# Sharing the start of a kernel out anew: first sequence's k and v in long runs, its p on ScalarE's queue, its mix on TensorE

## Chip, cores and metric

The kernel runs on one core of one Trainium2 chip. The metric is the device time of one execution in microseconds.

## What is computed

For each of 8 batches and 8 heads (S = 576 positions of D = 64) a packed attention, then a channel mix over the heads side by side (512 channels):

```python
def sm_attn(qq, kk, vv):                    # softmax(qq kk' / 8) vv
    ...
p_packed = sm_attn(p, k, v)                 # p: 32 rows a head
x = sm_attn(q, p_packed, p_packed)          # then heads side by side: [8, 576, 512]
x_prev = x shifted by one position, zero first
xk = mu_k * x + (1 - mu_k) * x_prev
xr = mu_r * x + (1 - mu_r) * x_prev
out = sigmoid(xr @ w_r) * (relu(xk @ w_k) ** 2 @ w_v)
```

The inputs mu and w are float64 and reach the chip as pairs of 32-bit words; q, k, v, p are float32. w_k is [512, 1024], w_v [1024, 512], w_r [512, 512].

## The kernel before, in words

A planner (`Flow`) runs generators with ranks and estimated times and emits the instructions in that order; the order on each engine is fixed when the kernel is built. Tiles come from pools with a set count of slots (`take`, `give`).

*Attention of one batch.* k and q arrive head by head, in pieces of 64 floats (256 bytes) for batches 0 and 1 (`loads`), are turned on TensorE (`transposed_on_pe`, L387) and copied to SBUF by ScalarE (kT, qT). p arrives in four loads (`packed`, L407) and is turned on VectorE (`pt`, L416). `front` makes the scores of p against k (L437); `weights_of` takes the maximum and exp and turns the result (L520, aT); L461 sums v with it; VectorE scales that to `pm`; its transpose ppT meets q in `back` (s2, L541). `back` ends with eight VectorE steps and exp (L553 to L576), of which a2 comes, and px (L584) is x transposed, 128 channels at a time; `mixed_in` copies it to `xt`.

*Channel mix.* Positions are cut into 9 chunks of 512. `mix` forms mu * x + (1 - mu) * x_prev, one scaled copy on ScalarE (L639), one scale-add on VectorE (L643); `split` makes a high and a low part (L659 on ScalarE, L661 on VectorE), so that three fast matmuls stand for one exact one. `gates` (L717 to L719) are 16 units of three matmuls, `keys` (L678 to L680) 32, `values` (L746 to L748) 32 per chunk.

*Weights.* `convert` loads a [128, 512] piece of float64 (SP, L207) into a `sq` slot, and turns it into a high and a low part: ScalarE scales the upper words (L285, `m`), VectorE shifts (L287), merges the sign (L289) and the low bits (L291), ScalarE casts the high part (L295), VectorE subtracts (L297). There are 4 pieces of w_r, 8 of w_k, 8 of w_v, 2.27 us of VectorE each. The parts of w_v have tiles of their own.

*The start.* TensorE has nothing but batch 0's attention until the first mix is done, and the planner fills it with matmuls on `spare` (L817). All loads go out on SP's queue, k of batch 0 first, then p, v, q, w_r. A load takes the semaphore of the eighth load before it, so that at most eight are in flight.

Of the kernel before, what the change touches and what calls it, by code (L numbers as in the profile page):

```python
# [163 lines left out]
def attn_pack_channel_mix(ctx: ExitStack, tc: tile.TileContext, q, k, v, p, mu_k, mu_r, w_k, w_v, w_r, out):  # L164
# [48 lines left out]
    LANDS = 2.0  # L213
    T6 = S // 6
# [49 lines left out]
    wv_h = const.tile([P, NF, DM], F32R, name="wv_h")  # L264
    wv_l = const.tile([P, NF, DM], F32R, name="wv_l")

    def convert(w, hi, lo, c, o, n, event, first=None):
# [4 lines left out]
        staged = yield from flow.take("staged")  # L272
        slot = yield from flow.take("sq")
        st = tile_([P, 2 * WP], U32, "sq", slot, "st")
        yield from load(st[:, :2 * n], w[c * P:(c + 1) * P, o:o + n].bitcast(U32), 0.46, 3.5e-3 * n)
# [93 lines left out]
    def transposed_on_pe(tag, b, pr, raw_space, raw_slot, raw):  # L369

        yield from reached()
        kq = yield from flow.take("kq")
# [473 lines left out]
```

## Time and profile before

| | us |
|---|---|
| median of 3 runs | 606.32 (605.44 to 607.43) |
| span of the profiled execution | 605.1 |
| TensorE busy in it | 593.7 |
| VectorE, ScalarE busy | 363.9, 331.0 |

The profile has no time of its own for the profiled execution beside its span; the median stands 1.2 us above the span. The busy time of TensorE counts `spare` matmuls, and ends of matmuls are modelled, so a busy stretch is read with its lines. Times in the rows are from the start of the span.

### The profile page before, as it was taken

Reading aid. Unit: us, or ns where it says so; the run is one execution under the profiler, and the core shown is the slowest. Engines: PE = TensorE matmul, PEld = TensorE weight load, DVE = VectorE, ACT = ScalarE, POOL = GpSimd, SP = SyncE. Lnnn points to the kernel's source line nnn. Section 1 sums busy time; section 2 is a strip of 40 time slices with the busy share of each in tenths; the row PEclk is TensorE's granted clock in tenths of the full one; section 3 lists DMA queues with packets and bytes.
Section 4 is the critical chain, followed back from the end, with each engine's and each line's share of the span. In section 5 each row is a group of like instructions: output and inputs, shape, how many; then the busy total and the mean of one; then the engine's idle time right before and its main releaser. Section 6 shows DMA issues by size and latency. Waiting matters only on the chain.

```text
span 605.1 us, 10174 instructions
## 1 busy us (share of the span) xinstructions
PE 593.7 (98%) x3984; PEld 471.1 (78%) x3984; DVE 363.9 (60%) x701; ACT 331.0 (55%) x579; POOL 2.1 (0%) x23
## 2 busy tenths in 40 slices
PE   8899999999999999999999999999999999999997
PEld 7787777777777777777877787778788888888886
DVE  1499999949688479556765577166503822451321
ACT  4478784775774648454845485457534803641420
POOL 0000000000000000000000000000000000000000
PEclk9899999999999999999999999999999999999999
DMA  8895561764634646346034702000010010001001
GB/s 189 248 266 136 216 155 34 166 126 88 113 60 137 118 70 139 99 74 143 1 103 64 144 1 72 20 1 0 26 45 1 0 70 0 2 0 71 0 2 69
DMA packets 159184, 49.43 MB, mean 82 GB/s; under 512 B 143776, under 2 KB 151968, under 8 KB 159136
## 3 DMA queue, kind: packets, MB, share of 16 engines
q1 hardware_dynamic: 159136, 48.79, 34.0%
q8 instruction: 31, 0.51, 0.3%
q14 instruction: 17, 0.14, 0.1%
HBM read 39.33 MB, written 9.44 MB: 81 GB/s over the span
## 4 chain that ended last, share of the span: by engine, by line
PE 84%; DVE 5%; ACT 4%; SPq 3%; DMA 2%; issue 1%; ACTq 0%
PE pvo L746 11%; PE ph L678 10%; PE pvo L747 10%; PE pvo L748 10%; PE ph L680 10%; PE ph L679 10%; PE pr L717 5%; PE pr L719 5%; PE pr L718 5%; SPq L207 3%; PE pa L461 2%; PE pa L584 2%; DMA st<-in_moe_w_r 1%; PE pa L541 1%; ACT x L639 1%; DVE m L289 1%
## 5 line engine op out<-in xcount | busy, mean ns | idle before, releaser
L678 PE MATMUL ph<-xk,wk_h 128*128 128x512 f32 x288 | 114.8, 399 | 0.0
L746 PE MATMUL pvo<-wv_h,sq 128*128 128x512 f32 x288 | 113.9, 395 | 0.0
L679 PE MATMUL ph<-xk,wk_h 128*128 128x512 f32 x288 | 112.4, 390 | 0.0
L680 PE MATMUL ph<-xk,wk_l 128*128 128x512 f32 x288 | 112.3, 390 | 0.0
L747 PE MATMUL pvo<-wv_l,sq 128*128 128x512 f32 x288 | 112.3, 390 | 0.0
L748 PE MATMUL pvo<-wv_h,sq 128*128 128x512 f32 x288 | 112.2, 390 | 0.0
L689 ACT ACTIVATE r<-ph 128x512 f32<-128x512 f32 x72 | 43.0, 598 | 90.7 <-PE ph L680 89.7
L696 DVE CAST sq<-r 128x512 fp32r<-128x512 f32 x72 | 30.3, 420 | 100.6 <-ACT r L692 98.4
L746 PEld LDWEIGHTS pvo<-wv_h,sq 128*128 128x128 f32 x288 | 54.1, 188 | 15.9 <-issue 4.5
L678 PEld LDWEIGHTS ph<-xk,wk_h 128*128 128x128 f32 x288 | 54.1, 188 | 15.5 <-issue 4.5
L643 DVE SCALAR_TENSOR_TENSOR x<-xt,mus,x 128x512 f32<-128x512 f32 (+7 forms) x128 | 60.4, 513 | 6.0 <-ACT x L639 5.9
L680 PEld LDWEIGHTS ph<-xk,wk_l 128*128 128x128 f32 x288 | 54.1, 188 | 11.5
L748 PEld LDWEIGHTS pvo<-wv_h,sq 128*128 128x128 f32 x288 | 54.1, 188 | 11.4
L639 ACT ACTIVATE x<-xt,mus 128x512 f32<-128x512 f32 (+7 forms) x128 | 62.0, 530 | 1.5 <-DVE xr L661 1.3
L747 PEld LDWEIGHTS pvo<-wv_l,sq 128*128 128x128 f32 x288 | 54.1, 188 | 10.7
L679 PEld LDWEIGHTS ph<-xk,wk_h 128*128 128x128 f32 x288 | 54.2, 188 | 10.3
L717 PE MATMUL pr<-wr_h,xr 128*128 128x512 f32 x144 | 58.7, 408 | 0.0
L719 PE MATMUL pr<-wr_h,xr 128*128 128x512 f32 x144 | 56.7, 394 | 1.0 <-DVE xr L661 1.0
L718 PE MATMUL pr<-wr_l,xr 128*128 128x512 f32 x144 | 56.3, 391 | 0.0
L728 ACT ACTIVATE sig<-pr 128x512 f32<-128x512 f32 x36 | 21.3, 601 | 60.1 <-PE pr L719 56.5
L698 DVE TENSOR_TENSOR sq<-r,sq 128x512 fp32r<-128x512 f32 x72 | 49.4, 686 | 1.4
L757 DVE TENSOR_TENSOR sig<-pvo,sig 128x512 f32<-128x512 f32 x36 | 23.9, 686 | 38.8 <-PE pvo L748 38.8
(80 smaller groups left out, 727.5 us busy)
## 6 DMA issues: line engine op xcount, KB each, us to landing
out<-sig SPq DMA_DIRECT2D x36, 256.0 KB, 2.1
vt<-in_v SPq DMA_DIRECT2D x16, 512.0 KB, 4.6
raw<-in_k SPq DMA_DIRECT2D x96, 72.0 KB, 2.8
raw<-in_q SPq DMA_DIRECT2D x96, 72.0 KB, 2.8
st<-in_moe_w_k SPq DMA_DIRECT2D x8, 512.0 KB, 6.0
st<-in_moe_w_v SPq DMA_DIRECT2D x8, 512.0 KB, 5.5
raw<-in_k SPq DMA_DIRECT2D x16, 144.0 KB, 2.9
raw<-in_q SPq DMA_DIRECT2D x16, 144.0 KB, 5.1
```

Of the source, the lines that this page charges most:

```text
L639: nc.scalar.mul(x32[:, o:o + n], xts[b, c][:, 1 + s:1 + s + n], mus[:, j, c:c + 1])
L643: nc.vector.scalar_tensor_tensor(x32[:, o:o + n], xts[b, c][:, s:s + n], mus[:, j + 1, c:c + 1], x32[:, o:o + n], op0=ALU.mult, op1=ALU.add,)
L678: nc.tensor.matmul(ph, wk_h[:, c, fs], xh, start=(c == 0), stop=False)
L679: nc.tensor.matmul(ph, wk_h[:, c, fs], xl, start=False, stop=False)
L680: nc.tensor.matmul(ph, wk_l[:, c, fs], xh, start=False, stop=(c == NC - 1))
L698: nc.vector.tensor_tensor(hl[:, 1, :], r, hl[:, 0, :].bitcast(F32), op=ALU.subtract)
L717: nc.tensor.matmul(pr, xh[:, ts_], wr_h[:, c, :], start=(c == 0), stop=False)
L718: nc.tensor.matmul(pr, xh[:, ts_], wr_l[:, c, :], start=False, stop=False)
L719: nc.tensor.matmul(pr, xl[:, ts_], wr_h[:, c, :], start=False, stop=(c == NC - 1))
L746: nc.tensor.matmul(pv[t], sh, wv_h[:, f, :], start=(f == 0), stop=False)
L747: nc.tensor.matmul(pv[t], sh, wv_l[:, f, :], start=False, stop=False)
L748: nc.tensor.matmul(pv[t], sl, wv_h[:, f, :], start=False, stop=(f == NF - 1))
```

## The change

Four things, all in the start. (1) k and v of batch 0 are loaded two heads at a time with six neighbouring positions to a partition, so in runs of 6 x 64 floats (1,536 bytes). VectorE puts k in the old order (`side`) ahead of the transposes, aT is made of six blocks of 96 to match v, and half of the qT copies move from ScalarE to VectorE. (2) w_r's first piece is loaded ahead of k, the second behind it; the four loads of batch 0's p and eight small new ones of mu (`mub`) go out on ScalarE's queue. (3) Batch 0's first chunk is no longer mixed on ScalarE and VectorE: mu goes into `pm` (`shared`: `pms`, two taps for each of xr and xk), and TensorE makes xr and xk directly from A (a2 with a zero column ahead, kept in halves hf = 0, 1), eight groups of eight matmuls; ScalarE casts the high part and VectorE subtracts, both from PSUM (`first_out`). The 64 positions left over are `kept` for the next chunk. Gates and keys wait for halves (`made`). (4) Weight pieces have eight `st` slots; w_v's two parts are written over the piece they came from. Conversions of w_k are `held` until both halves of A are there.

```diff
-    FIRST = 10.09, 10.29
+    FIRST = 9.97, 9.982, 10.07, 10.09
-    def load(dst, src, issue, us):
+    def load(dst, src, issue, us, beside=False):
+        if beside:
+            yield "scalar", 0.1, None, None
+            nc.scalar.dma_start(dst, src)
+            return
...
+                if b == 0 and tag == "kT":
+                    raw = tile_([P, 2, 6, D], F32, space, slot, "raw")
+                    yield from load(
+                        raw[:T6], src[b, 2 * pr:2 * pr + 2].rearrange("h (p c) d -> p h c d", p=T6), 0.4, 0.76,
+                    )
...
+            r2 = tile_([P, 6, 2 * D], F32, "raw", side, "side")
+            yield vec2(12 * D)
+            nc.vector.tensor_copy(r2[:T6].rearrange("p c (h d) -> p h c d", h=2), raw[:T6])
...
-            if beside:
+            if beside and hf:
                 yield act(HS)
                 nc.scalar.copy(t[:, hf * HS:(hf + 1) * HS], bank[:, :HS])
+            elif beside:
+                yield vec(HS)
+                nc.vector.tensor_copy(t[:, hf * HS:(hf + 1) * HS], bank[:, :HS])
...
+    def shared(sp, pm):
...
+        for j in (1, 0):
+            nc.vector.tensor_tensor(pms[:, j, 0], flat, mub[1][:, j], op=ALU.mult)
+            nc.vector.tensor_tensor(pms[:, j, 1], flat, pms[:, j, 0], op=ALU.subtract)
...
+    def first_mix():
...
+                        for pr in (2 * g, 2 * g + 1):
+                            own = slice(32 * pr, 32 * pr + 32)
+                            for h, half in enumerate(HALVES):
+                                o = 1 - tap + hf * HS
+                                nc.tensor.matmul(
+                                    px[half, pr % 2, :HS], pms[own, j, tap, h * D:(h + 1) * D], A[own, h, o:o + HS],
+                                    start=(tap == 0), stop=(tap == 1),
+                                )
...
+    def first_out(tag, j, hf, g, slot, px, tiles, kept):
+            nc.scalar.copy(tiles[c][:, 0, cols], px[:, c % 2, :n])
+            nc.vector.tensor_tensor(tiles[c][:, 1, cols], px[:, c % 2, :n], tiles[c][:, 0, cols].bitcast(F32), op=ALU.subtract)
...
-                nc.tensor.matmul(pv[t], sh, wv_h[:, f, :], start=(f == 0), stop=False)
+                nc.tensor.matmul(pv[t], sh, wvs[f][:, 0, :], start=(f == 0), stop=False)
```

The order on ScalarE at the start of the program. Before (L254 is a warm-up, L396 copies kT, L510 is the exp, L526 copies aT):

```order
L254 ACT_TABLE_LOAD
L254 ACTIVATE warm<-warm 128x1
L396 COPY kT<-pa 128x576 x4
L510 ACTIVATE a,sm<-pa,nmx 128x576 x2
L526 COPY aT<-pa 128x512
```

Now (L209 issues a load, L288 is the old L285, L436 the old L396, L302 the old L295):

```order
L209 DMA pin<-in_p 32x4x32
L260 ACT_TABLE_LOAD
L260 ACTIVATE warm<-warm 128x1
L209 DMA mub<-in_moe_mu_k 32x128
L209 DMA pin<-in_p 32x4x32
L209 DMA mub<-in_moe_mu_k 32x128
L209 DMA pin<-in_p 32x4x32
L209 DMA mub<-in_moe_mu_k 32x128
L209 DMA pin<-in_p 32x4x32
L209 DMA mub<-in_moe_mu_k 32x128
L209 DMA mub<-in_moe_mu_r 32x128 x4
L288 ACTIVATE m<-st 128x512
```

Twelve loads now stand ahead of the first conversion, and the conversion ahead of the first copy of kT.

VectorE between `pm` and the second softmax. Before (L476 is pm, then a weight piece, then s2):

```order
L476 TENSOR_TENSOR pm<-pa,rs 128x128
L287 TENSOR_SCALAR m<-m 128x512
L289 SCALAR_TENSOR_TENSOR m<-st,m 128x512
L291 SCALAR_TENSOR_TENSOR m<-st,m 128x512
L553 STREAM_TRANSPOSE e<-pa 128x576 x2
```

Now (L524 is pm, L290 to L294 are L287 to L291, L678 and L680 make pms, L615 is the old L553):

```order
L524 TENSOR_TENSOR pm<-pa,rs 128x128
L290 TENSOR_SCALAR m<-m 128x512
L292 SCALAR_TENSOR_TENSOR m<-st,m 128x512
L294 SCALAR_TENSOR_TENSOR m<-st,m 128x512
L678 TENSOR_TENSOR pms<-pm,mub 128x128
L290 TENSOR_SCALAR m<-m 128x512
L680 TENSOR_TENSOR pms<-pm,pms 128x128
L292 SCALAR_TENSOR_TENSOR m<-st,m 128x512
L615 STREAM_TRANSPOSE e<-pa 128x576 x2
```

Between the two stand two shifts, three merges and two halves of `pms` where one shift and two merges stood.

TensorE from the end of the attention to the gates. Before (L584 is px, L717 to L719 are one unit of the gates):

```order
L584 MATMUL pa<-a_544,pm 64x288 x8
L817 MATMUL spare<-ident 128x128 x4
L387 MATMUL pa<-ident,raw 128x96 x6
L817 MATMUL spare<-ident 128x128 x18
L717 MATMUL pr<-wr_h,xr 128x512
L718 MATMUL pr<-wr_l,xr 128x512
L719 MATMUL pr<-wr_h,xr 128x512
L817 MATMUL spare<-ident 128x128 x4
L717 MATMUL pr<-wr_h,xr 128x512
L718 MATMUL pr<-wr_l,xr 128x512
L719 MATMUL pr<-wr_h,xr 128x512
```

Now (L711 is a group of the mix, two of them in the first row; L871 to L873 are a unit of the gates):

```order
L423 MATMUL pa<-ident,raw 128x96 x6
L711 MATMUL pa<-A_444,pms 64x288 x16
L984 MATMUL spare<-ident 128x128 x9
L711 MATMUL pa<-A_444,pms 64x288 x8
L871 MATMUL pr<-wr_h,xr 128x512
L872 MATMUL pr<-wr_l,xr 128x512
L873 MATMUL pr<-wr_h,xr 128x512
L871 MATMUL pr<-wr_h,xr 128x512
L872 MATMUL pr<-wr_l,xr 128x512
L873 MATMUL pr<-wr_h,xr 128x512
L711 MATMUL pa<-A_444,pms 64x288 x8
```

The filler between px and the gates is gone but for nine matmuls, and groups of the mix stand among the units of the gates.

## Rows read from the trace of the kernel before

**Rows 1.** The page's first lines: the span, and each engine's busy time, share of the span and instructions.
```profile
span 605.1 us, 10174 instructions
PE 593.7 (98%) x3984; PEld 471.1 (78%) x3984; DVE 363.9 (60%) x701; ACT 331.0 (55%) x579; POOL 2.1 (0%) x23
```

**Rows 2.** Timeline of TensorE around the first gates and keys: start us, us, engine, line, operation, out<-in, sizes, count of records (a full-precision matmul leaves two) and, in brackets, the idle time ahead and what ended it.
```profile
44.67 0.48 PE L717 MATMUL pr<-wr_h,xr 128*128 128x512 f32 x1
...
48.56 2.39 PE L817 MATMUL spare<-ident 128*128 128x128 f32 x20
...
61.57 0.39 PE L678 MATMUL ph<-xk,wk_h 128*128 128x512 f32 x1
...
64.06 0.39 PE L680 MATMUL ph<-xk,wk_l 128*128 128x512 f32 x1
...
70.56 1.21 PE L437 MATMUL pa<-kT,pt 64*32 64x288 f32 x32 [1.34 <-DVE pt L416]
```

**Rows 3.** Table of stages: stretch (us from the start of the span), its length, busy us and instructions of PE, PEld, DVE, ACT and POOL, granted TensorE clock (1.00 is 2.4 GHz), DMA share, GB/s.
```profile
40.00:50.00 10.00, 9.02 (x73) 8.06 (x72) 9.93 (x17) 9.82 (x19) 0.00 (x0) 1.00 0.99 267
...
70.00:80.00 10.00, 9.44 (x77) 7.41 (x78) 9.90 (x22) 8.80 (x17) 0.00 (x0) 1.00 0.41 128
```

**Rows 4.** Timeline of SP's queue: start us, us, the issues and their count.
```profile
0.73 4.24 SPq L207 DMA_DIRECT2D raw<-in_k  x8
```

**Rows 5.** Loads to landing: for batch 0's k and p the line, count, KB each and median us from issue to landing; then, for all weight pieces issued in 0:80, the least, median and most.
```profile
raw<-in_k SPq DMA_DIRECT2D x8, 144.0 KB, 2.8
pin<-in_p SPq DMA_DIRECT2D x4, 16.0 KB, 2.1
DMA to landing us min/median/max: 3.3/6.2/8.4
```

**Rows 6.** Table of stages, for the rates of loads: only k in 3:6, only q in 17:19, mostly w_r in 25:27; the last two columns are DMA share and GB/s.
```profile
3.00:6.00 3.00, 3.00 (x24) 3.00 (x24) 0.00 (x0) 0.27 (x1) 0.00 (x0) 1.00 1.11 251
17.00:19.00 2.00, 2.00 (x50) 1.79 (x49) 0.00 (x0) 1.36 (x4) 0.00 (x0) 0.80 1.11 235
25.00:27.00 2.00, 2.00 (x19) 2.00 (x20) 2.00 (x4) 0.62 (x1) 0.00 (x0) 1.00 1.07 385
```

**Rows 7.** Chain of waits, 7 to 24 us: start us, us, what. The two issues of q that were held longest in SP's queue.
```profile
10.74 1.32 SPq L207
...
12.10 3.03 SPq L207
```

**Rows 8.** Groups of ScalarE's instructions by line and shape up to 110 us: names, shapes, count | busy us, mean ns | idle time ahead and releasers.
```profile
L285 ACT ACTIVATE m<-st 128x512 f32<-128x512 f32 x20 | 13.6, 684 | 3.8 <-DMA st<-in_moe_w_r 2.5 <-DMA st<-in_moe_w_k 0.7 <-ACT m L285 0.6
...
L396 ACT COPY kT<-pa 128x576 f32<-128x576 f32 x8 | 5.0, 637 | 4.6 <-PE pa L387 4.4
...
L526 ACT COPY aT<-pa 128x512 f32<-128x512 f32 x4 | 2.3, 585 | 0.7 <-PE pa L461 0.5 <-PE pa L521 0.3
```

**Rows 9.** Timeline of VectorE through batch 0's second softmax.
```profile
21.66 0.29 DVE L476 TENSOR_TENSOR pm<-pa,rs 128x128 f32<-128x128 f32 x1 [7.68 <-PE pa L461]
...
25.32 1.44 DVE L553 STREAM_TRANSPOSE e<-pa 128x576 f32<-128x576 f32 x2
...
29.30 0.17 DVE L793 TENSOR_SCALAR mus<-mus 128x8 f32<-128x8 f32 x1
...
30.53 1.41 DVE L566 TENSOR_REDUCE z<-e 128x18 f32<-128x576 f32 x2
...
36.98 0.77 DVE L576 STREAM_TRANSPOSE a<-e 128x576 f32<-128x576 f32 x1
```

**Rows 10.** Timeline of VectorE, later: the mix (L643, L661), and the steps of one weight piece between those of its neighbours.
```profile
46.21 0.75 DVE L643 SCALAR_TENSOR_TENSOR x<-xt,mus,x 128x512 f32<-128x512 f32 x1
46.88 0.69 DVE L661 TENSOR_TENSOR xk<-x,xk 128x512 fp32r<-128x512 f32 x1
...
57.67 0.42 DVE L287 TENSOR_SCALAR m<-m 128x512 uint32<-128x512 uint32 x1
...
58.74 0.68 DVE L297 TENSOR_TENSOR wk_l<-m,wk_h 128x512 fp32r<-128x512 f32 x1
59.34 0.68 DVE L291 SCALAR_TENSOR_TENSOR m<-st,m 128x512 uint32<-128x512 uint32 x1
59.94 0.42 DVE L287 TENSOR_SCALAR m<-m 128x512 uint32<-128x512 uint32 x1
```

**Rows 11.** Timeline of TensorE through batch 0's attention.
```profile
9.15 1.20 PE L437 MATMUL pa<-kT,pt 64*32 64x288 f32 x32
...
16.65 0.44 PE L387 MATMUL pq<-ident,raw 96*128 96x96 f32 x3 [2.15 <-DMA raw<-in_q]
17.02 0.65 PE L461 MATMUL pa<-vt,aT 128*32 128x64 f32 x32
...
20.14 1.08 PE L461 MATMUL pa<-vt,aT 128*32 128x64 f32 x32
...
23.70 1.20 PE L541 MATMUL pa<-qT,ppT 64*32 64x288 f32 x32
...
38.54 0.74 PE L584 MATMUL pa<-a,pm 32*64 32x288 f32 x16
```

**Rows 12.** Table of stages, single microseconds: the clock is the third column from the right.
```profile
18.00:19.00 1.00, 1.00 (x8) 0.98 (x8) 0.00 (x0) 0.96 (x3) 0.00 (x0) 0.60 1.16 232
...
20.00:21.00 1.00, 1.00 (x34) 0.84 (x32) 0.00 (x0) 0.56 (x2) 0.00 (x0) 0.50 0.98 355
```

More of the change, by code (lines that the diff above doesn't have):

```diff
@@ L213, in attn_pack_channel_mix @@
     LANDS = 2.0
+    WLOAD = 2.6e-3
     T6 = S // 6
@@ L271, in convert @@
             flow.now.rank = first
[L272 to L275, printed above, removed]
+        slot = yield from flow.take("st")
+        st = tile_([P, 2 * WP], U32, "st", slot)
+        yield from load(st[:, :2 * n], w[c * P:(c + 1) * P, o:o + n].bitcast(U32), 0.46, WLOAD * n)
         flow.now.rank = rank
         yield from reached()
+        if held:
+            yield from flow.wait(("A", 1))
         sm = yield from flow.take("tmp")
@@ L348, in values_of @@
     def values_of(b, h):
+        if b == 0:
+            slots, vt = [], []
+            for j in range(2):
+                slots.append((yield from flow.take("sq")))
+                vt.append(tile_([P, 2, 6 * D], F32, "sq", slots[j], "vt"))
+                yield from load(
+                    vt[j][:T6], v[b, 4 * j + h:4 * j + h + 3:2].rearrange("h (p c) d -> p h (c d)", p=T6), 0.4, 0.76,
+                )
+                if not j:
+                    back_to_issue()
+            vts[b, h] = slots, vt, None
+            flow.set(("vt", b, h))
+            return
         slot = yield from flow.take("vt")
@@ L629, in mix @@
         for c in range(NC):
-            yield from flow.wait(*(("xt", b, c, hf) for b, *_ in pieces(i) for hf in range(2)))
+            yield from flow.wait(*(("xt", b, c, hf) for b, *_ in pieces(i) if b for hf in range(2)))
             slot = yield from flow.take("xk" if tag == "xk" else "sq")
-            space = "sig" if i == 0 else "tmp"
+            space = "tmp"
             sx = yield from flow.take(space)
@@ L666, in attn_pack_channel_mix, with made @@
     sqs, sigs = {}, {}
+    def made(tag, i, c, t=NT - 1):
+        if i:
+            return [(tag, i, c)]
+        return [(tag, 0, c, hf) for hf in range(1 + ((t + 1) * P > HS))]
     def keys(i):
@@ L673, in keys @@
             for c in range(NC):
-                yield from flow.wait(("xk", i, c), ("wk", c, f * P // WP * WP))
+                yield from flow.wait(*made("xk", i, c), ("wk", c, f * P // WP * WP))
                 yield pe(0.69)
@@ L712, in gates @@
             for c in range(NC):
-                yield from flow.wait(("xr", i, c), *(("wr", c, o) for o in range(0, DM, WP)))
+                yield from flow.wait(*made("xr", i, c, t), *(("wr", c, o) for o in range(0, DM, WP)))
                 yield pe(0.69)
@@ L785, in all_loads @@
             yield from loads(b)
+    mub = []
     def shares():
+        sm = yield from flow.take("sig")
+        mub[:] = sm, tile_([P, 2, 2 * D], F32, "sig", sm, "mub")
+        for j, mu in ((0, mu_k), (1, mu_r)):
+            for pr in range(NPR):
+                yield from load(
+                    mub[1][32 * pr:32 * pr + 32, j, :],
+                    mu[2 * D * pr:2 * D * (pr + 1)].unsqueeze(0).broadcast_to([32, 2 * D]), 0.46, 0.05, beside=True,
+                )
+        flow.now.t += 2.5
+        flow.set("mub")
         for j, mu in ((0, mu_k), (2, mu_r)):
@@ L802, in weights @@
             for c in range(NC):
[L803 removed]
+                flow.spawn(convert(w_k, wk_h, wk_l, c, o, WP, ("wk", c, o), held=True), RANK_W)
         for f in range(NF):
             for o in range(0, DM, WP):
[L806 removed]
+                flow.spawn(convert(w_v, None, None, f, o, WP, ("wv", f, o)), RANK_V)
     flow.spawn(all_loads(), 10)
```

174 lines of the change are left out of this document (135 added, 39 removed).

## The prediction

> **What bounds the kernel now.** I read the page's busy line first, then the table of stages, then the queues in order of time. The page has TensorE busy in 593.7 of a span of 605.1 us [rows 1]. That number hides the start, where the `spare` matmuls count as busy: until the first gate matmul at 44.67 us TensorE does only batch 0's attention and filler, and 20 more filler records follow at 48.56 [rows 2]. The table of stages shows who is full there: VectorE is busy 9.93 of 10 us in 40:50 and 9.90 in 70:80, ScalarE 9.82 in 40:50 [rows 3]. From the first key matmul at 61.57 us TensorE runs nearly without a gap; the one visible stall is 1.34 us ahead of L437 at 70.56, where batch 1's `pt` stands late in VectorE's queue [rows 2]. So the kernel is a start of about 60 us, bounded by batch 0's attention chain and then by VectorE, and 540 us of TensorE. The change touches the first part. My measure is the end of the keys' first chunk (f = 0, four c): before, 64.06 + 0.39 = **64.45 us** [rows 2].
>
> **Part 1: the loads.** SP issues a load in about 0.5 us (8 in 4.24) [rows 4]; the first k pieces land 2.8 us after issue, p's 2.1, a weight piece 3.3 at best [rows 5]. Now w_r's first piece goes first and lands at 0.73 + 3.3 = 4.0. k and v of batch 0 become eight loads of 295 KB in runs of 1,536 bytes. No row has such runs. The nearest are k in runs of 256 bytes, 251 GB/s, and weight rows of 4 KB, 385 GB/s [rows 6]: 1.18 or 0.77 us each. I take 0.77, since the weights' runs are long ones too; at the other end the eight cost 3.3 us more. The Trainium skill (DMA: Bandwidth & Descriptors, the opening table, "Min transfer for line-rate") puts the knee at 512 bytes; by it 0.77 holds, and without it the sum below would be 1.9 us later. Then: k lands by 7.1, w_r's second piece (524 KB at 385: 1.36) 8.5, v by 12, q (eight of 147 KB at 235: 0.6 each) 16.8, the two `mus` about 18.2, w_r's other two by 22.1, seven w_k pieces by 31.7, batch 1's p 32. Nothing below waits longer for those last ones: `pt` of batch 1 stands in VectorE's queue where it arrives at about 33.6.
>
> **Part 2: twelve loads on ScalarE's queue.** They stand ahead of its first conversion. Five go at once, seven wait for earlier loads (eight are in flight at most over both queues). No row shows a load issued there; SP's rows are the nearest, 0.43 to 0.5 us, and 1.32 or 3.03 when an issue is held up [rows 4, 7]. With 0.5: the sixth waits for w_r's first piece (4.0), so ScalarE is free at 4.0 + 7 x 0.5 + 0.3 = 7.8. At 1.32 for the seven: 13.5.
>
> **Part 3: batch 0's front comes later.** From 7.8: `m` 0.6 [rows 8]; then on VectorE one shift, four `side` copies and two merges before the fourth pair of k is in order. A copy of 768 has no row; by the shift of 512 (0.42) and the transpose of 576 (0.72) [rows 9, 10] it lies between 0.5 and 1.0, I take 0.5 as for the shift. That is 0.4 + 2.0 + 1.2, so 12.0. Transposes 0.5, ScalarE's cast, `m` and two copies in its queue 0.5 to 0.64 each [rows 8]: the scores start at 14.0, where they started at 9.15 [rows 11]. **4.9 us late.**
>
> **Part 4: and catches up.** Before, the next steps stood still for q: TensorE idles 2.15 us to 16.65, and `pm` comes at 21.66 [rows 9, 11]. Now q lands by 16.8 and v by 12. Scores 14.0 to 15.2, VectorE (with the second w_r conversion ahead) 15.9 to 17.8 for two maxima and a qT half, second exp to 19.0, six transposes 0.8, aT copy 0.8 (0.585 for 512 [rows 8]), second sum 0.9 as in L461's rows, waits of 0.2: `pm` at 22.3, s2 at 23.1 against 23.70. In VectorE's queue seven instructions of w_r's last pieces and `pms` now stand between `pm` and the transposes of s2, 3.2 us: these begin at **25.5, against 25.32** [rows 9]. So the front gains nothing itself; what is gained is that w_r's conversions are done (about 5 us of VectorE's work moved into its idle first 22 us).
>
> **Part 5: to A.** From 25.5: two transposes, maxima and subtractions 4.0 (25.32 to 29.30 before), sums 1.33, `pms`, one wr_l, small ones, one merge, products, and four half transposes for two whole ones. A(0) at 35.2, A(1) at 36.6. The old second a2 ends at 36.98 + 0.77 = 37.75 [rows 9]. **1.2 us earlier.**
>
> **Part 6: the mix.** Out go eight scale-adds (0.67 from start to start) and eight subtractions of 512 (0.60) on VectorE [rows 10], 10.2 us, with their partners on ScalarE. In come 16 subtractions from PSUM, of 288 and 224; by a slope between `pm`'s 128 (0.29) and 512 (0.69) 0.37 and 0.30, 5.4 us [rows 9, 10]. On TensorE a group is eight matmuls in two accumulating taps on half the array; one wave over the whole array is 0.74 (L584), two waves 1.2 (L437) [rows 11]. I take 1.05 for a lone group. From 36.6 VectorE needs 40 instructions to the last xk: 5.4 + 5 wk_l and 7 each of the others of a conversion (2.27 a piece from start to start [rows 10]) 14.0 + 1.1 where one waits for its own forerunner = 20.5, and 1.0 waiting for groups: 58.1. TensorE's first lone group waits until the PSUM pair is drained at 38.4; then 16 gate units of 0.69, five more groups, batch 1's k transposes 1.2, one key chunk 2.76: 11.0 + 6.3 + 1.2 + 2.8 = 21.4, so 59.8, and 0.5 of waits: **60.3 us. That is 4.1 earlier.** TensorE is now behind VectorE by a little. With a group at 0.74 VectorE ends it at 59.0, with 1.2 TensorE at 61.2.
>
> **Part 7: after that.** The same key, value and gate work. The 1.34 us stall goes, since `pt` of batch 1 is done near 34; what is late next is batch 1's fourth kT, whose copy stands behind a wk_h cast on ScalarE: 0.5. Transposes of k that were made in filler time add 0.2. Net 0.6 to 0.7 saved. The four qT halves on VectorE (0.37 each) cost nothing, since it idles before `pm` anyway (7.68 us before [rows 9]). w_v split in place costs nothing either: same instructions, slots freed by w_k in time, and VectorE is further ahead of TensorE than before; with that cover gone each of the eight pieces would hold the values by up to 2.27.
>
> **Sum.** 4.1 + 0.7 = 4.8 us. The profiled span of 605.1 becomes 600.3. The runs' median, 606.32, stands 1.2 above that span; I add it: **601.5 us**. Its own range, with a group at 0.74 to 1.2, copies and waits either way: 598.4 to 604.
>
> **Rivals.**
> - *TensorE runs at the low level through the front.* In the trace of before the 2.15 us of idleness ahead of 16.65 is followed by a granted clock of 0.60 and 0.50 (0.50 is 1.2 GHz, 1.00 2.4) in 18:19 and 20:21, and a sum that takes 0.65 takes 1.08 [rows 11, 12]. The change opens wider gaps: filler ends near 6, `side` comes at 9.4. Transposes, sums and half of the scores doubled cost 1.6 us ahead of `pm`: 603.1. The Trainium skill (TensorE: Matmul & The Clock Gate, "HAM oscillation") says such gaps bring the clock down; the trace agrees by those rows. For it: the gaps. Against: s2 has slack behind VectorE. 0.14.
> - *k and v land no faster* (251 GB/s): w_r's last piece lands 3.3 us later, `m` and ppT behind it in ScalarE's queue, e 1.9 later: 603.4. Against: the weights' rate. 0.10.
> - *VectorE is not relieved*: if a 288 or 224 from PSUM takes the 0.69 of a 512, 16 of them cost 11.0 instead of 5.4, VectorE ends the xk at 63.7 and the chunk ends at 64.6: 605.8, no change. Against: `pm`'s 0.29 for 128. 0.11.
> - *Slower: ScalarE's queue is held by its loads.* If the seven that wait are held like the worst two of SP, (1.32 + 3.03) / 2 = 2.2 us each [rows 7], ScalarE is free at 4.0 + 15.4 + 0.3 = 19.7, 11.9 later, and kT, s1 and all behind them with it: 613. It decides from about 1.4 us each, where the 4.8 and 1.8 more are gone. For it: kT's copies stand right behind. Against: these loads are small (16 KB or less), SP's held ones were 144 KB. 0.11.
>
> **Chances.** The forecast has 0.54. About 0.3% (1.8 us) is what a measurement of this kernel can tell from no change. Faster by more: 0.54 + 0.14 + 0.10 = 0.78; within: 0.11; slower: 0.11. The range takes in the forecast, the first two rivals and the edge of the third: 598.4 to 605.0.
>
> **What would show it.** ScalarE's first `m` near 8 us; scores near 14; s2's transposes on VectorE near 25.5; the last transposition of A near 36; gates from about 39.5 with no filler among them; the first key chunk done near 60; no wait for `pt` in batch 1. The forecast is wrong if the first `m` comes after 11, if VectorE idles long between 36 and 58, if a lone group takes 2 us, or if TensorE shows new gaps of some us after 62.

## The result: 0.65% slower, where 0.8% faster was forecast

The changed kernel takes 610.14 us (median of 6 runs, 609.71 to 613.48); the kernel before, run beside it, 607.44. The ratio is **1.0065**, 95% interval 1.0042 to 1.0087. The profiled execution has a span of 607.7 us and a time of 609.75; the span of before was 605.1 [rows 1], that of the forecast 600.3.

My measure, the end of the keys' first chunk, stood at 64.45 before, was forecast at 60.3 and came at 67.84 + 0.40 = **68.24**. TensorE, timeline (start us, us, line, operation, [idle ahead and what ended it]), to set beside [rows 2, 11]:

```profile
10.33 1.43 PE L423 MATMUL pa<-ident,side 96*128 96x96 f32 x12 [3.82 <-DVE side L405]
...
12.24 2.17 PE L423 MATMUL pa<-ident,side 96*128 96x96 f32 x12
...
15.74 1.20 PE L479 MATMUL pa<-kT,pt 64*32 64x288 f32 x32
...
27.12 1.20 PE L603 MATMUL pa<-qT,ppT 64*32 64x288 f32 x32 [1.06 <-ACT ppT L533]
...
38.48 0.69 PE L423 MATMUL pa<-ident,raw 96*128 96x96 f32 x6 [1.25 <-DMA raw<-in_k]
...
45.07 0.50 PE L871 MATMUL pr<-wr_h,xr 128*128 128x512 f32 x1
...
57.89 0.39 PE L873 MATMUL pr<-wr_h,xr 128*128 128x512 f32 x1
58.21 1.20 PE L711 MATMUL pa<-A,pms 32*64 32x288 f32 x16
59.34 0.50 PE L871 MATMUL pr<-wr_h,xr 128*128 128x512 f32 x1
...
63.88 0.47 PE L423 MATMUL pa<-ident,raw 96*128 96x96 f32 x3 [0.84 <-ACT kept L729]
...
67.84 0.40 PE L834 MATMUL ph<-xk,wk_l 128*128 128x512 f32 x1
```

The scores (L479) start at 15.74, forecast 14.0; s2 (L603) at 27.12, forecast 23.1, after a wait for ppT. From 45.07 to 63 TensorE has no gap, and a lone group of the mix (L711) puts 1.45 us between two gates (57.89, 59.34) that are 0.23 apart elsewhere: the stage belongs to TensorE, which e11 below puts to the test. VectorE, the steps of [rows 9]:

```profile
8.07 0.31 DVE L458 STREAM_TRANSPOSE pt<-pin 128x128 f32<-128x128 f32 x1 [8.07 <-DMA pin<-in_p]
...
18.42 0.46 DVE L432 COPY qT<-pq 128x288 f32<-128x288 f32 x1 [0.62 <-PE pq L423]
...
24.27 0.29 DVE L524 TENSOR_TENSOR pm<-pa,rs 128x128 f32<-128x128 f32 x1 [0.38 <-PE pa L508]
25.70 0.43 DVE L290 TENSOR_SCALAR m<-m 128x512 uint32<-128x512 uint32 x1 [1.14 <-ACT m L288]
...
28.84 1.44 DVE L615 STREAM_TRANSPOSE e<-pa 128x576 f32<-128x576 f32 x2
...
38.26 0.31 DVE L458 STREAM_TRANSPOSE pt<-pin 128x128 f32<-128x128 f32 x1 [1.31 <-DMA pin<-in_p]
...
40.81 0.47 DVE L638 STREAM_TRANSPOSE A<-e 128x288 f32<-128x288 f32 x1
```

`pm` is 2.0 late against the forecast (24.27 for 22.3). s2's transposes (L615) are 3.3 late: behind `pm` VectorE waits 1.14 for the conversion of w_r's third piece. The last transposition of A is 4.7 late (41.28 for 36.6; the old a2 ended at 37.75): ahead of it stands `pt` of batch 1, which waits 1.31 for its load. ScalarE:

```profile
8.69 0.66 ACT L288 ACTIVATE m<-st 128x512 f32<-128x512 f32 x1 [6.01 <-DMA mub<-in_moe_mu_r]
...
25.00 0.67 ACT L288 ACTIVATE m<-st 128x512 f32<-128x512 f32 x1 [1.36 <-DMA st<-in_moe_w_r]
26.25 0.67 ACT L288 ACTIVATE m<-st 128x512 f32<-128x512 f32 x1 [0.58 <-DMA st<-in_moe_w_r]
26.82 0.25 ACT L533 COPY ppT<-pa 128x128 f32<-128x128 f32 x1
```

The copy of ppT, which s2 needs, stands behind two conversions that wait for w_r's third and fourth piece. The table of stages (clock, DMA share, GB/s are the last three columns):

```profile
12.00:15.00 3.00, 3.00 (x19) 2.92 (x18) 2.57 (x5) 2.89 (x6) 0.00 (x0) 0.50 1.07 278
20.50:22.00 1.50, 1.50 (x23) 1.32 (x25) 0.46 (x1) 1.44 (x5) 0.00 (x0) 1.00 0.28 14
...
45.00:63.00 18.00, 18.00 (x132) 11.08 (x128) 15.35 (x33) 12.14 (x27) 0.10 (x1) 1.00 0.64 196
```

In 12:15 nearly all that moves is v in runs of 1,536 bytes: 278 GB/s, not the 385 of weight rows. In 45:63 TensorE is busy all 18 us and VectorE 15.35; before, VectorE was the full one [rows 3].

k is late for another reason. Its third and fourth piece are issued at 4.91 and 6.85 only; SP's queue stands still for landings of p, which goes out on ScalarE's queue, since at most eight loads are in flight. SP's queue, and what it waits for in 0:12 (us in total, times, longest):

```profile
1.18 0.91 SPq L212 DMA_DIRECT2D raw<-in_k  x2
...
4.91 2.25 SPq L212 DMA_DIRECT2D raw<-in_k  x2
7.25 0.40 SPq L212 DMA_DIRECT2D st<-in_moe_w_r  x1
```
```profile
SPq L212 <- DMA pin<-in_p: 4.8, 3, 2.8
```

### The profile page after: what moved, and what is told of

Its sections match the earlier page's. It is cut to its first block, busy times and chain, and to the rows that moved or that the text cites. A ratio compares the mean times of both kernels' runs of the same rounds, so it can differ in the third digit from the quotient of the medians.

```text
span 607.7 us, 10264 instructions
## 1 busy us (share of the span) xinstructions
PE 594.3 (98%) x4028; PEld 467.1 (77%) x4028; DVE 364.4 (60%) x707; ACT 323.0 (53%) x573; POOL 2.2 (0%) x22
## 4 chain that ended last, share of the span: by engine, by line
PE 90%; DMA 5%; DVE 2%; SPq 1%; ACT 1%; issue 0%; ACTq 0%; DVEq 0%
PE pvo L900 11%; PE ph L832 11%; PE pvo L901 11%; PE pvo L902 11%; PE ph L833 10%; PE ph L834 10%; PE pr L871 6%; PE pr L872 5%; PE pr L873 5%; PE pa L508 2%; DMA pin<-in_p 2%; PE pa L656 2%; DMA st<-in_moe_w_k 1%; PE pa L711 1%; SPq L212 1%; PE pa L603 1%
## 5 line engine op out<-in xcount | busy, mean ns | idle before, releaser
L900 PE MATMUL pvo<-wv,sq 128*128 128x512 f32 x288 | 113.6, 395 | 0.0
L901 PE MATMUL pvo<-wv,sq 128*128 128x512 f32 x288 | 112.2, 390 | 0.0
L902 PE MATMUL pvo<-wv,sq 128*128 128x512 f32 x288 | 112.1, 389 | 0.0
L900 PEld LDWEIGHTS pvo<-wv,sq 128*128 128x128 f32 x288 | 54.0, 188 | 15.6 <-issue 4.1
L902 PEld LDWEIGHTS pvo<-wv,sq 128*128 128x128 f32 x288 | 54.1, 188 | 11.4
L901 PEld LDWEIGHTS pvo<-wv,sq 128*128 128x128 f32 x288 | 54.1, 188 | 10.7
L871 PE MATMUL pr<-wr_h,xr 128*128 128x512 f32 x144 | 59.2, 411 | 0.0
L787 DVE SCALAR_TENSOR_TENSOR x<-xt,mus,x 128x448 f32<-128x448 f32 (+6 forms) x112 | 53.1, 513 | 9.6 <-ACT x L781 9.4
L873 PE MATMUL pr<-wr_h,xr 128*128 128x512 f32 x144 | 56.2, 391 | 0.0
L781 ACT ACTIVATE x<-xt,mus 128x448 f32<-128x448 f32 (+6 forms) x112 | 54.3, 530 | 1.9 <-DVE xr L809 1.8
```

The source lines that it names most:

```text
L781: nc.scalar.mul(x32[:, o:o + n], xts[b, c][:, 1 + s:1 + s + n], mus[:, j, c:c + 1])
L787: nc.vector.scalar_tensor_tensor(x32[:, o:o + n], xts[b, c][:, s:s + n], mus[:, j + 1, c:c + 1], x32[:, o:o + n], op0=ALU.mult, op1=ALU.add,)
L871: nc.tensor.matmul(pr, xh[:, ts_], wr_h[:, c, :], start=(c == 0), stop=False)
L873: nc.tensor.matmul(pr, xl[:, ts_], wr_h[:, c, :], start=False, stop=(c == NC - 1))
L900: nc.tensor.matmul(pv[t], sh, wvs[f][:, 0, :], start=(f == 0), stop=False)
L901: nc.tensor.matmul(pv[t], sh, wvs[f][:, 1, :], start=False, stop=False)
```

## Experiments

All are edits of the changed kernel, five rounds each beside the kernel before. Ratios have 95% intervals; event times are from one profile each, "low" is a granted clock of 0.50 (1.2 GHz) between 35 and 55 us. e15 and e18 have the same order up to A and differ by 0.8 at `pm` and at A; the changed kernel and e11 too, and differ by 1.35 at the scores and 0.5 at A. So a difference of 0.8 or less at A is not told from this spread.

| | ratio | scores | s2 on VectorE | last A done | first gate | key chunk done | low | span |
|---|---|---|---|---|---|---|---|---|
| before | | 9.15 | 25.32 | 37.75 | 44.67 | 64.45 | no | 605.1 |
| after | 1.0065 (1.0042-1.0087) | 15.74 | 28.84 | 41.28 | 45.07 | 68.24 | no | 607.7 |
| e1 | 1.0227 (1.0198-1.0255) | 14.73 | 27.16 | 39.21 | 44.52 | 71.63 | yes | 617.9 |
| e2 | 1.0199 (1.0166-1.0232) | 11.18 | 26.05 | 38.49 | 43.12 | 66.95 | yes | 612.7 |
| e3 | 1.0079 (1.0058-1.0099) | 16.45 | 28.95 | 41.49 | 49.23 | 69.72 | yes | 609.6 |
| e4 | 1.0128 (1.0107-1.0148) | 15.65 | 29.35 | 40.15 | 48.92 | 72.09 | yes | 612.1 |
| e5 | 1.0095 (1.0064-1.0125) | 15.64 | 28.16 | 41.46 | 47.28 | 70.49 | no | 610.0 |
| e6 | 1.0137 (1.0111-1.0164) | 17.14 | 29.73 | 44.70 | 50.04 | 73.21 | yes | 612.6 |
| e7 | 1.0114 (1.0082-1.0145) | 16.76 | 28.93 | 43.90 | 48.11 | 71.31 | no | 610.8 |
| e8 | 1.0087 (1.0058-1.0115) | 16.50 | 26.95 | 38.07 | 50.20 | 72.38 | yes | 611.9 |
| e9 | 1.0189 (1.0169-1.0208) | 17.01 | 30.21 | 41.53 | 45.53 | 68.70 | no | 617.0 |
| e10 | 1.0218 (1.0190-1.0247) | 15.80 | 28.51 | 38.29 | 45.23 | 71.50 | yes | 617.0 |
| e11 | 1.0016 (1.0001-1.0032) | 17.09 | 28.62 | 40.76 | 43.58 | 64.31 | no | 603.9 |
| e12 | 1.0098 (1.0081-1.0115) | 14.62 | 28.09 | 41.63 | 47.56 | 70.73 | yes | 611.5 |
| e13 | 1.0063 (1.0039-1.0087) | 16.33 | 28.07 | 40.25 | 44.03 | 67.20 | no | 607.6 |
| e14 | 1.0022 (1.0008-1.0037) | 16.44 | 26.73 | 37.85 | 42.25 | 65.40 | no | 605.5 |
| e15 | 0.9996 (0.9984-1.0008) | 14.77 | 26.01 | 37.13 | 41.51 | 64.66 | no | 604.7 |
| e16 | 1.0012 (1.0000-1.0024) | 14.80 | 27.14 | 38.26 | 42.53 | 65.65 | no | 605.7 |
| e17 | 1.0100 (1.0075-1.0124) | 14.33 | 28.20 | 39.89 | 43.99 | 66.55 | no | 612.0 |
| e18 | 1.0109 (1.0089-1.0128) | 14.84 | 26.84 | 37.97 | 42.31 | 66.14 | yes | 617.2 |

**The mix back on ScalarE and VectorE (e3).** `mixes(i)` as before for chunk 0, from a2 and xt.

> The change with the first chunk mixed as before the change (scaled copy, scale-add, high and low part on ScalarE and VectorE); the mu loads on ScalarE's queue are still made, and not used. Theory M: TensorE loses six groups of 1.4 us among its gates, the first key chunk ends near 65 instead of 68.2 and the time falls by 3 us. Theory L: a2 comes as late as A did (near 41.5), VectorE has 4.8 us more to do, the chunk ends near 68 to 69, the time is the change's within 1 us.

Last A at 41.5, the chunk at 69.7: the old mix, 3.4 us of it at the low level, takes 28.2 us from there, the new one 27.0. The kernel before took 26.7 (37.75 to 64.45). So the mix on TensorE is not what makes the change slower; what comes ahead of it is. But it gains nothing either, where the forecast had 23.7.

**Fewer loads on ScalarE's queue (e1, e2, e6, e13).** e1 and e2 give the loads to SP through the planner, which then orders other things anew:

```diff
-  ... 0.46, 0.05, beside=True)       # e1: the mu rows; e2: p as well
+  ... 0.46, 0.05)
```

> The eight mu loads go on SP's queue behind w_r's last pieces; ScalarE issues p's four alone. Theory L (the two queues' loads wait for each other, eight in flight, and ScalarE and VectorE stand behind the landings): k's last load lands at about 8.5 instead of 9.8, w_r's last near 23 instead of 26.2, A is done near 38.5 instead of 41.3, the first key chunk ends near 65.5 instead of 68.2; about 2.7 us faster than the change. Theory M (the mix in lone groups on TensorE is what costs): no more than 0.5 us.

> As before, and p's four loads too go on SP's queue, behind w_r's second piece; ScalarE issues none. Theory L: ScalarE's first m near 5 instead of 8.7, scores near 13 instead of 15.7 (p lands near 11), first key chunk near 65; about 3 us faster than the change. Theory M: no more than 0.5 us.

In e2 the scores come 4.6 us earlier, but the last A only 2.8: `pm` comes at 20.48, then VectorE waits for w_r's third piece (1.16) and for the second `mus` load (1.69). e2 is still 1.3 ahead of the changed kernel at the chunk's end and loses it later, with new gaps of TensorE at 124 to 133; e1 is behind at the chunk's end, with two stretches at the low level, and has gaps at 127 to 138. e6 keeps every order and moves only the issues to SP; e13 leaves the mu loads out:

```diff
-            nc.scalar.dma_start(dst, src)
+            late[beside].append((dst, src))   # e6: issued on SP behind k, behind w_r
+            nc.gpsimd.memset(dst, 0.5)        # e13: instead of the mu loads
```

> The changed kernel with its order on every engine as it is, but the twelve loads of p and of the two mu rows issued on SP's queue (p's four behind batch 0's k, the mu's eight behind w_r's fourth piece) and none on ScalarE's. Theory L (loads of the two queues wait for one another and hold ScalarE): first m at 4.5 instead of 8.7, scores at 11 to 12 instead of 15.7, s2's transposes on VectorE at 26 instead of 28.8, last transposition of A at 38.5 instead of 41.3, the first key chunk done at 65.5 to 66 (1.5 more if the clock falls to 0.5 in the gate stage), span 605 to 606.5. Rival (the front is bounded by landings of q, v and w_r's last two pieces, which stand behind four more issues on SP): scores earlier, but s2's transposes within 0.5 of 28.8 and the span 607 to 608.5.

> The changed kernel with the eight loads of the mu rows left out (GpSimd fills the two tiles with 0.5 instead), so that ScalarE's queue has p's four loads alone; order as it is on every other engine. Theory L (these eight hold ScalarE and stand between the loads of p and k): first m at 4.5 to 5 instead of 8.7, p landed at 6 to 7 instead of 8.0, k at 8.8 instead of 9.8, scores at 14 to 14.5, s2's transposes at 27.3 to 28, span 606 to 607. Rival (w_r's late pieces and batch 1's p and k set the end of the front, and they land as late): scores earlier, last A within 0.5 of 41.3, span 607.2 or more.

e13 decides for the eight mu loads: ScalarE is free at 4.66 instead of 8.69 and k's last piece is issued at 4.88 instead of 6.85. But p's last load lands at 8.38 and k's at 10.41 (8.00 and 9.78 in the changed kernel), k's among w_r's second piece, which is issued 0.36 behind it; so `pt` comes at 8.50 and the scores at 16.33 (with 6.8 us of low clock ahead of them instead of 3.4). Last A comes 1.0 earlier, the ratio is the same. Theory L falls for the mu loads; p's four stay on ScalarE's queue in e13. In e6 the four loads of p behind k put `pt`, and all of VectorE's queue behind it, 1.5 us later, and batch 1's p held A for 3.85.

**Filler and planner's costs (e5, e7, e9, e10).**

```diff
+  for _ in range(14): flow.fill()    # e5, e7: ahead of batch 1's first transposes; 6 ahead of the mix
-  ..., p=T6), 0.4, 0.76,             # e9, e10: k and v
+  ..., p=T6), 0.45, 1.1,
```

> The changed kernel with 20 more spare matmuls on TensorE, 14 ahead of the transposes of batch 1's first k (where TensorE stood idle 1.25 us in the profile of the changed kernel) and 6 ahead of the first group of the mix; nothing else moves. Theory C (in most executions TensorE's idleness ahead of the mix brings its granted clock to 0.5 in the gate stage, as it did with 1.6 us idle or more in the four runs before): no 0.5 after 16 us in the profile, and the median falls from 610 to 608 or a little below, close above the span. Rival (the executions without a profile are slower for another reason): the profile stays at 607.7 +- 0.5 and the median at 610. Rival (filler stands in the way): 0.5 to 1 us slower in both.

> The loads on SP's queue as in the run before, and the 20 spare matmuls as well. Theories L and C together: no 0.5 in the gate stage, first key chunk done near 65.5, span 605, median 605.5: the level of the kernel before, no better, since s2 and the mix gain nothing. If only L holds: as the run before. If the clock's fall in the gate stage is what costs most: over 2 us below the run before.

My mistake in e5: a filler leaves two records of 0.115 us, and I counted one. 14 take 3.2 us where 1.25 was idle, and the first gate comes 2.2 later. Where the idleness was longer, e7 against e6, the same filler removed the low level and brought the chunk's end 1.9 forward, 0.8 of it there at A already.

> The changed kernel with the same instructions, but ordered by the planner with the loads' times as the trace of the changed kernel shows them (k and v 1.1 us each instead of 0.76, p's and the mu's small loads 0.18 and 0.16 and 0.45 of ScalarE each instead of 0.1, p landed at 7.6 and the mu's at 14.3 instead of some 3 and 5). The planner then has the last transposition of A at 37.4 (33.9 with the change's numbers, 41.3 in the trace), ppT ahead of the conversions of w_r's last two pieces, batch 1's p behind the transpositions of A and its k behind the mix, and more filler ahead of the mix. Theory P (the change's gain is lost because its order was planned on loads that come 5 to 8 us earlier than they do, and each queue then waits for the late one): scores at 15.2 to 15.7, s2's transposes at 27 to 28, last A at 38.5 to 39.5, no wait for batch 1's p or k ahead of the mix, no 0.5 in the gate stage, first key chunk done at 64 to 65.5, span 603 to 605, median 605 to 607. Rival (the loads themselves are what is late, order or not): last A at 40 to 41 and the first key chunk at 67 to 68, median 609 to 610.

> As the run before it, with the mu's eight loads on SP's queue among w_k's pieces, so that only p's four loads are left on ScalarE's. Theory (the loads on ScalarE's queue hold k's, and ScalarE itself until 8.7): first m at 4.8, pt of batch 0 at 5 to 6 instead of 8, scores at 13.5, s2's transposes at 26, last A at 37 to 38 (the planner has 35.0), first key chunk done at 62.5 to 64, span 601.5 to 603.5. Rival (q's and w_r's landings bound the front, whatever stands on ScalarE): scores earlier, but s2's transposes and A within 0.5 of the run before it.

Theory P falls: with the loads' measured times A still comes at 41.5 (e9). The wait for batch 1's p is gone (from s2's transposes to A 11.3 us instead of 12.4), but `pm` comes at 25.68, 1.4 later, and s2 stands behind q's transposes. Later w_v's loads pass batch 1's last ones, and TensorE waits 1.62 and 1.86 us at 124 and 129 and is at the low level from 127.7 to 134.5. e10 brings A to 38.29, near what its theory said, with the conversions ordered anew as well, so that the runs don't tell which of the two did it. It loses more behind A: 6.9 us to the first gate, the low level from 45.4 to 52.2, gaps at 127 to 135.

**What stands ahead of A and the mix (e4, e8, e14).** e4 loads batch 1's p ahead of w_k; e8 holds w_r's late conversions; e14 holds batch 1's k too:

```diff
+        if first and first > 10:
+            yield from flow.wait(("ppT", 0))     # e8, e14: w_r's third and fourth piece
+        if b == 1 and tag == "kT":
+            yield from flow.wait("mixing")       # e14: set by the mix's fourth group
```

> Batch 1's p is loaded ahead of w_k instead of behind its seventh piece. Theory L: VectorE's wait of 1.31 us at 38.26 for it is gone, A is done about 1 us earlier, and the first key chunk with it; 0.8 to 1.3 us faster than the change, since TensorE still waits for batch 1's k until 38.5 ahead of the mix. Theory M: nothing.

> The changed kernel with the conversions of w_r's third and fourth piece held until batch 0's ppT is copied (the planner then orders the rest anew). Theory (ppT stands behind two conversions on ScalarE that wait for w_r's late pieces, and s2's transposes behind their followers on VectorE): ppT at 24.8 instead of 26.8, s2 at 25.1, s2's transposes on VectorE at 26 instead of 28.8, last A at 39 to 40 with the conversions' 3.2 us of VectorE coming in later; first key chunk done at 66 to 67 instead of 68.2, span 606 to 607, unless TensorE idles over 1.5 us ahead of the mix, when the gate stage at 0.5 takes it back. Rival (VectorE has the same work before A in either order): ppT earlier, A within 0.5 of 41.3, span 607.7.

> The changed kernel with the conversions of w_r's third and fourth piece held until ppT is copied, as in the eighth run, and the transposes of batch 1's k held until the first half of the mix is issued. Theory (what holds A and the mix are queues behind late loads: ppT behind the two conversions, the transpositions of A behind batch 1's p, the mix behind batch 1's k): s2's transposes at 27, last A at 38 instead of 41.3, no idleness over 1.5 us ahead of the mix and no 0.5 in the gate stage, gates from 41.8, first key chunk at 65 to 65.7, span 604.3 to 605.3, median 606 to 607: the kernel before's level. Rival (A earlier, but TensorE at 0.5 again in the gate stage): span 607 to 610. Rival (VectorE, with the conversions later, takes it back): first key chunk at 67 or later without any 0.5.

e4 and e8 bring A as early as expected or earlier (40.15, 38.07), and lose it: TensorE's queue then stands still for batch 1's k (2.11 and 2.19 us), and its clock falls. e8, TensorE, and e4's stage 42:49:

```profile
37.53 0.69 PE L425 MATMUL pa<-ident,raw 96*128 96x96 f32 x6 [2.19 <-DMA raw<-in_k]
...
41.91 2.20 PE L714 MATMUL pa<-A,pms 32*64 32x288 f32 x16
```
```profile
42.00:49.00 7.00, 7.00 (x55) 4.96 (x43) 3.79 (x8) 3.65 (x8) 0.00 (x0) 0.57 1.02 295
```

A group takes 2.20 where it took 1.20. In e8 the time of one and the same kernel goes with its mean clock: 608.1 us in the two executions at 0.994, 611.0 at 0.991, 612.6 to 614.6 in the six at 0.986 to 0.989. e14 takes all three late loads away at once (`pt` of batch 1 goes behind A by the planner's new order) and lands where it was expected. Its VectorE and TensorE:

```profile
36.07 0.82 DVE L643 STREAM_TRANSPOSE A<-e 128x288 f32<-128x288 f32 x2
36.82 0.65 DVE L306 TENSOR_TENSOR wr_l<-m,wr_h 128x512 fp32r<-128x512 f32 x1
37.39 0.47 DVE L643 STREAM_TRANSPOSE A<-e 128x288 f32<-128x288 f32 x1
```
```profile
37.06 1.25 PE L716 MATMUL pa<-A,pms 32*64 32x288 f32 x32
...
42.25 0.50 PE L878 MATMUL pr<-wr_h,xr 128*128 128x512 f32 x1
```

No wait stands ahead of A and the first two groups; last A 3.4 us earlier than in the changed kernel, the chunk 2.8, the median 2.65 (607.49).

**The size of the mix's groups (e11).**

```diff
-                    for tap in range(2):
+                    for tap in range(1):
```

> The changed kernel with one of the two accumulating taps of the first chunk's mix left out (four matmuls instead of eight a group, the other operand's product is missing); order and everything else as it is. Theory T (in the gate stage TensorE is the bound, through the mix's lone groups at 1.45 us from the matmul before to the matmul after, where the forecast had 1.05): a group then costs 0.9, the gate stage falls from 18.0 to about 15.3, the first key chunk is done at 65 to 65.7 instead of 68.2, span 604.7 to 605.5, median 607 to 607.6. Rival (VectorE is not relieved and bounds the stage): first key chunk at 67.5 or later, span 607 or more.

```profile
54.95 0.39 PE L873 MATMUL pr<-wr_h,xr 128*128 128x512 f32 x1
55.27 0.71 PE L711 MATMUL pa<-A,pms 32*64 32x288 f32 x8
55.91 0.50 PE L871 MATMUL pr<-wr_h,xr 128*128 128x512 f32 x1
```

A group now takes 0.96 from gate to gate instead of 1.45, the gate stage 15.5 instead of 18.0, and from the last A to the chunk's end it takes 23.55 us instead of 26.96. Theory T holds; VectorE, with the same work, was not the bound.

**The clock in the front (e12, e15), w_r's pieces (e16, e17), the last version (e18).**

```diff
+            if b == 0 and tag == "kT" and pr == hf == 0:
+                for _ in range(16): flow.fill()     # e12; e15 to e18 on top of e14
-    FIRST = 9.97, 9.982, 10.07, 10.09
+    FIRST = 9.97, 10.05, 10.07, 10.09               # e16; e17: 9.981, 10.05, ...
```

> The changed kernel with 16 more spare matmuls (about 3.4 us) ahead of the transposes of batch 0's first k, where TensorE stands idle 3.8 us; nothing else moves. Theory (this idleness brings the granted clock to 0.5 from 12 to 15 us, and the transposes and scores of that time run at half speed): no 0.5 before 16 us, scores at 14.8 to 15 instead of 15.7, s2's transposes 0.5 to 0.8 earlier, span 607, median 609 to 609.5. Rival (VectorE's copies pace the transposes, the clock costs nothing): scores within 0.2 of 15.7, no change.

```profile
12.30 1.48 PE L426 MATMUL pa<-ident,side 96*128 96x96 f32 x12
...
14.62 1.57 PE L482 MATMUL pa<-kT,pt 64*32 64x288 f32 x32
```

The second twelve transposes take 1.48, not 2.17: the low clock cost 1.1 us at the scores. Nothing of it is left at `pm` (24.62, in the changed kernel 24.27), since TensorE then waits 1.24 for q. s2's transposes come 0.75 earlier, as w_r's fourth piece does (converted at 25.55 instead of 26.25). Batch 1's k again took it back (2.05 us idle, low from 39.3 to 46.1).

> The kernel of the run e14 with the 16 spare matmuls of e12 ahead of batch 0's transposes as well. Theory (each of the causes found costs by itself): no 0.5 in the first 600 us, scores at 14.6 instead of 16.4, s2's transposes at 26 to 26.5 (26.7 in e14, since q's landing holds VectorE's queue from 18 to 24 anyway), last A 37.2 to 37.8, span 604.8 to 605.5, median 606.5 to 607.3. Rival (what the scores gain reaches A in full): last A at 36, span 603.7.

e15, all of it together: 606.95 us, ratio 0.9996. That is 3.2 us less than the changed kernel and level with the one before. Against e14 it is 0.5 us, and the intervals of the two ratios just touch.

> As e15, with w_r's second piece (512 KB) loaded behind batch 0's q instead of ahead of v and q. Theory (w_r's pieces ahead of v and q make q land later, and VectorE's qT copies, which stand ahead of the maxima and of pm, wait for it): q landed by 19.5 to 20.5 instead of 20.6 to 22.2, pm at 23 instead of 24.6, s2's transposes at 25, last A at 36.5, unless the conversion that now comes later costs VectorE 2.4 us after pm; span 603.5 to 605, median 605.5 to 606.7. Rival (q lands as late, for another reason): pm within 0.4 of e15's.

> As e16, with w_r's first piece loaded behind batch 0's k. Theory: k landed by 8.5 to 8.8 instead of 9.8 to 10.2, p's four within 7 to 8.2, scores at 13 to 13.5, s2's transposes at 24.5, last A at 36, one conversion more behind pm; span 603 to 604.5, median 605 to 606.3: at or a little below the kernel before. Rival (what VectorE converts later it lacks in the front and the mix): last A at 37 or later, span 605 or more.

Both are slower than e15, the opposite of what I expected: e16 by 0.7 us, e17 by 6.7. In e16 q lands by 19.9, as expected, but `pm` comes at 25.2 in e16 and 25.3 in e17 (23.9 in e15). w_r's second piece now stands ahead of the two small `mus` loads in SP's queue, and VectorE stands still for the second of them ahead of `pm`, in e16 and e17:

```profile
23.03 0.17 DVE L970 TENSOR_SCALAR mus<-mus 128x8 f32<-128x8 f32 x1 [1.54 <-DMA mus<-in_moe_mu_r]
```
```profile
24.24 0.17 DVE L970 TENSOR_SCALAR mus<-mus 128x8 f32<-128x8 f32 x1 [3.06 <-DMA mus<-in_moe_mu_r]
```

In e15 this wait is 0.62. The conversion that now stands between it and `pm` adds its steps. Of e17's 6.7 us only 1.9 are there at the chunk's end; the rest comes later, with gaps of TensorE at 121 to 129 and 3.4 us at the low level. So whether loading w_r early pays is not shown: the wait for `mus` was not taken away.

> The kernel of e15 with five of the eleven spare matmuls between the mix's second and third group left out (in e15's trace they run until 40.24, while the slot that the third group needs is drained at 39.46) and with the transposes of batch 1's k held until the keys' first chunk is issued (in e15 they stand 0.84 us ahead of the first key matmul, waiting for a slot that ScalarE's `kept` frees). Theory: gates from 40.7 instead of 41.5, first key matmul at 59 instead of 60.55, first key chunk done at 62 to 62.6 instead of 64.66, of which batch 1's transposes take 1.2 back later; span 603 to 603.8 and median 605 to 605.8, a little below the kernel before. Rival (batch 1's front, now some 3 us later, comes late for its gates, or the loads behind its raw slots do): gaps of TensorE between 90 and 130, span 604.5 or more.

The expectation rested on a misreading: the slot is not drained before 41, so fewer fillers left TensorE idle for 1.22 us, the clock fell for 6.8 us, and batch 1 came late (gaps at 124 to 132). No version here beats the kernel before.

## Why the prediction was wrong

**Part 1, the loads, failed.** k was to land by 7.1 and landed by 9.78, v 17.1 instead of 12, q 22.2 instead of 16.8, w_r's last piece 26.2 instead of 22.1, batch 1's p 37.7 instead of 32 (landings in the trace). Of the 5.1 us at v, 2.7 are there at k: I used the limit of eight loads in flight for ScalarE's queue in part 2 and forgot it for k on SP's. Another 1.8 came at w_r's second piece (3.2 us behind k instead of 1.4), and 0.6 at v itself: its four pieces take 4.2 us where 3.5 was left for them, landing 0.9 to 1.2 apart, where 0.77 was put. The rate lies between my two ends, 278 GB/s in 12:15; in e2, where nothing holds k's issues, k alone moves at 306 in 4:7. I named the low end as a rival and priced it as 1.9 us of e (the start of s2's transposes), without its effect further on. The Trainium skill (DMA: Bandwidth & Descriptors, the opening table) has the line rate from 512 bytes on. A stretch that I didn't look at, in the kernel before, agrees: there v alone moves, in runs of 1,024 bytes to 128 partitions, at 375 GB/s. Runs of 1,536 bytes at 278 to 306 do not agree, and the measurement decides. They go to 96 partitions, and no run here parts that from the length. The stretches in before and e2 (the last two columns are DMA share and GB/s):

```profile
9.00:10.00 1.00, 1.00 (x35) 0.52 (x33) 0.00 (x0) 0.00 (x0) 0.00 (x0) 1.00 1.08 375
```
```profile
4.00:7.00 3.00, 2.59 (x21) 2.21 (x21) 1.50 (x4) 0.67 (x1) 0.00 (x0) 1.00 1.03 306
```

**Part 2 was near in its price** (0.32 to 0.47 us an issue on ScalarE, free at 8.69, forecast 7.8), and the rival built on it wrong: in e13 ScalarE is free 4 us earlier and the time stays.

**Parts 3 to 5, from k to A, 4.7 us late, failed as sums without queues.** I followed each engine's work and not what stands first in its queue waiting for a load. The 4.7 come in three steps: 2.0 at `pm`; 1.3 from there to s2's transposes (4.6 us instead of 3.2), where ppT and VectorE's next steps stand behind w_r's late conversions; 1.3 from there to A (12.4 instead of 11.1), which is the wait for batch 1's p. e14 takes away the last two and has A 3.4 earlier, at 37.85, forecast 36.6. e15's 37.13 is no further than single profiles differ. Why `pm` is 2.0 late was not parted further; e2, with scores and q earlier, has it at 20.48. The sentence "Nothing below waits longer for those last ones" is the one that broke.

**Part 6, the mix, 3.3 us late.** VectorE is relieved as forecast (subtractions at 0.37 and 0.30 from start to start), so it is not the third rival. The first gate comes 3.8 after the last A instead of 2.9. In the gate stage, 1.7 over the sum (18.0 for 16 units and five groups), the mis-sized term is the lone group: it adds 1.32 us (1.45 from gate to gate, less the 0.23 between two gates without one, plus 0.10 for the slower matmul behind it) instead of 1.05, five times, 1.4. Another 0.7 comes behind it, with a wait of 0.84 for `kept` where 0.5 was put for all waits. Since it leaves the bound with TensorE, each tenth of it counts. VectorE's count there adds to 21.2 and not 20.5 (the steps of [rows 10] give 14.7 where it has 14.0); TensorE's end was the later one either way.

**Part 7 was right:** from the chunk's end to the end of the span 539.5 us, before 540.65; 0.6 to 0.7 was forecast, 1.2 came. The 1.2 us from the span to the time is 2.05 in the changed kernel (607.7, 609.75).

Of the four signs of being wrong that I named none came; that A could be late was not among them.

**The clock rival** was right in kind: low from 11.9 to 15.3. Its price of 1.6 ahead of `pm` was too high: e12 shows 1.1 at the scores and nothing at `pm`. I did not look for it ahead of the mix. From the last A to the chunk's end the runs with the new mix that are low there take 28.2 to 34.3 us, the waits around it included; the changed kernel takes 27.0.

## What to carry to other kernels

When a change moves loads, follow every in-order queue to the first instruction that needs a late load, and count what stands behind it on that engine, however small. A gain in one wait is only worth what the next late load in the same queue leaves of it (e4, e8, e16); take them away together before judging any of them. And where filler is counted ahead of time, count it for the arrival, not for the plan.

## What the runs showed of the hardware that I had not expected

- Runs of 1,536 bytes to 96 partitions load at 278 to 306 GB/s, runs of 256, to 96 as well, at 251 [rows 6]; runs of 1,024 to 128 partitions reach 375, rows of 4 KB 349 to 385.
- While SP's issue of the second `mus` load (single 4-byte elements) is held, 19.25 to 20.87, no load behind it is issued, and the DMA moves 14 GB/s from 20.5 to 22; what holds it was not tried.
- TensorE's granted clock fell to 0.50 around the mix after idleness of 1.22 us (e18), 1.35 (e10), 1.6 (e2), 2.1 (e4, e12), 2.2 (e1, e8), and not after 1.25 (changed kernel) or 1.15 (e7): no single length tells the two apart.
- The mean clock goes with the spread of the runs: e15, at a mean clock of 0.998 to 1.000, lies within 606.5 to 607.8; the changed kernel, at 0.988 to 0.997, within 609.7 to 613.5.
